# Issuing a transformer block's projections and FFN between the exponentials of its attention

## The chip, the cores and the metric

One core of one Trainium2 chip runs the whole block. The metric is device time in microseconds (us); lower is better. Executions of one kernel lay within about 0.5% of their median, and medians are quoted.

## The reference, cut to what matters

```python
B, S, D, H, F = 1, 2048, 512, 32, 1792        # head size 16, bf16 inputs
h  = x + attention(layernorm(x)) @ wo          # softmax over 2048 keys, 32 heads
h2 = h + (sigmoid(ln(h) @ w_gate) * (ln(h) @ w_up)) @ w_down
```

The scores are 32 x 2048 x 2048, and each needs one exponential. That is 2048 tiles of 128 keys by 512 queries, issued three at a time: 683 ScalarE instructions of 128x1536 elements (the last one shorter), in both kernels.

## The kernel before

Three stages follow each other. The first makes K, Q and V for everything, 128 rows at a time, through padded tiles and TensorE transposes. The second is attention (some lines cut):

```python
pt_next = emit_scores(groups[0])          # 3 score matmuls (K=32, row tiles), then exp -> pt
for gi, group in enumerate(groups):
    pt = pt_next
    if gi + 1 < len(groups):
        pt_next = emit_scores(groups[gi + 1])
    for ui, (qc, g, kt, j) in enumerate(group):
        nc.tensor.matmul(acc[32*j:32*j+32, :], lhsT=Vaug[:, kt, 4*g+j, :], rhs=pt[:, ui, :],
                         start=(kt == 0), stop=(kt == NT-1), tile_position=(0, 32*j))   # "AV"
        if kt == NT - 1 and j == 3:       # end of a head group's 512 queries: normalise
            nc.vector.tensor_copy(out=xs[:], in_=acc[:])
            nc.tensor.matmul(pr[:], lhsT=sel_f[:], rhs=xs[:], start=True, stop=True)    # fp32, L215
            nc.vector.reciprocal(out=rec[:], in_=pr[:])
            nc.gpsimd.tensor_tensor(out=QT[g][:, qs], in0=xs[:], in1=rec[:], op=ALU.mult)
```

On TensorE the order is: scores n+1, AV n, scores n+2, AV n+1. AV n needs exponential n. The third stage does the output projection and second layer norm of all rows and then the FFN, with `Sqrt` and `Sigmoid` on ScalarE; the trace shows the two partly interleaved.

## Time and profile before

| | before |
|---|---|
| time | 1452.25 us (4 runs, 1450.85 to 1453.69) |
| start to first exponential | 233.1 us |
| first to last exponential | 1011.2 us |
| last exponential to end | 204.8 us |
| mean TensorE clock between first and last exponential | 0.52 |

The prediction shows the lines behind this. The ends of the stages are start and end times of the exponentials' own records. In a row of the list of groups, the figures after the first bar are busy time and mean length of one instruction; those after the second are idle time just before and what ended it.

### The profile page before, as it was taken

The numbers are of one execution on the slowest core, as the hardware profiler recorded it, in microseconds if no ns is written. First come the engines' busy times: TensorE is split into PE (matmuls) and PEld (weight loads), VectorE is DVE, ScalarE is ACT, GpSimd is POOL, SyncE is SP. The second block draws the span as 40 slices with busy tenths as digits, with TensorE's granted clock in tenths as the row PEclk, the third lists the DMA queues.
The fourth block names the chain that finished last, engine by engine and source line by source line (L and its number), as shares of the span: only waits on it lengthen the run. The fifth ranks groups of instructions, "written<-read, shape, count | busy, mean of one in ns | idle before, by whom it ended". The sixth has DMA issues, their size and how long they took to land.

```text
span 1449.1 us, 13593 instructions
## 1 busy us (share of the span) xinstructions
PE 1142.7 (79%) x5512; PEld 358.9 (25%) x5539; DVE 323.8 (22%) x546; ACT 1054.5 (73%) x863; POOL 131.6 (9%) x128
## 2 busy tenths in 40 slices
PE   1665556888888888888888888888888888699998
PEld 0332222222222222222222222222222222234444
DVE  8533331111111111111111111111111111356433
ACT  1111116999999999899999989999998999456221
POOL 7442220000000000000000000000000000000000
PEclk9998765555555555555555555555555555699999
DMA  3000000000000000000000000000000000400000
GB/s 116 1 1 0 0 0 1 1 0 0 1 0 1 1 0 1 0 0 1 0 0 1 0 1 0 1 1 0 1 0 1 1 0 0 153 1 0 23 23 15
DMA packets 6670, 12.66 MB, mean 9 GB/s; under 512 B 400, under 2 KB 4496, under 8 KB 6608
## 3 DMA queue, kind: packets, MB, share of 16 engines
q1 hardware_dynamic: 4896, 6.03, 1.2%
q10 hardware_dynamic: 1056, 3.41, 0.7%
q0 software_dynamic: 656, 2.36, 0.6%
q8 instruction: 43, 0.70, 0.2%
q14 instruction: 19, 0.16, 0.0%
HBM read 9.70 MB, written 2.10 MB: 8 GB/s over the span
## 4 chain that ended last, share of the span: by engine, by line
ACT 59%; PE 27%; DVE 8%; issue 5%; POOL 1%; another core or an unknown queue 0%; ACTq 0%; DVEq 0%; POOLq 0%
ACT pt L193 56%; PE pm L113 5%; PE pr L215 5%; PE pm L263 3%; PE pf L251 3%; PE acc L206 3%; PE pf L254 3%; PE pm L228 2%; DVE xs L213 2%; POOL sq L120 1%; PE pss L189 1%; DVE sel_f L57 1%; PE pm L167 1%; PE pm L85 1%; DVE KT L87 1%
## 5 line engine op out<-in xcount | busy, mean ns | idle before, releaser
L193 ACT ACTIVATE pt<-pss 128x1536 bf16<-128x1536 f32 (+1 forms) x683 | 944.8, 1448 | 66.4 <-PE pss L189 66.4
L206 PE MATMUL acc<-pt,Vaug 128*32 128x512 bf16 x2048 | 418.3, 592 | 163.7 <-ACT pt L193 163.7
L189 PE MATMUL pss<-QT,KT 32*128 32x512 bf16 x2048 | 408.3, 592 | 0.7 <-ACT Vaug L172 0.7
L206 PEld LDWEIGHTS <-Vaug 128*32 128x32 bf16 x2048 | 133.4, 101 | 468.9 <-issue 468.9
L213 DVE COPY xs<-acc 128x512 f32<-128x512 f32 x32 | 22.1, 691 | 822.9 <-PE acc L206 822.9
L189 PEld LDWEIGHTS <-KT 32*128 32x128 bf16 x2048 | 71.7, 99 | 300.1 <-issue 299.2
L218 POOL TENSOR_TENSOR QT<-xs,rec 128x512 bf16<-128x512 f32 x32 | 40.4, 1264 | 961.0 <-DVE rec L217 961.0
L217 DVE RECIPROCAL rec<-pr 128x512 f32<-128x512 f32 x32 | 107.4, 3357 | 69.5 <-PE pr L215 69.5
L113 PE MATMUL pm<-wqkv_sb,xnT 128*128 128x512 bf16 x183 | 80.2, 599 | 17.1 <-DVE xnT L87 15.7
L257 ACT ACTIVATE sg<-pf 128x512 f32<-128x512 f32 x56 | 32.7, 596 | 70.1 <-PE pf L251 60.2
L215 PE MATMUL pr<-xs,sel_f 128*128 128x512 f32 x64 | 65.8, 1131 | 9.5 <-DVE xs L213 9.5
L75 ACT ACTIVATE rstd<-mv,eps_t 128x1 f32<-128x1 f32 x32 | 9.4, 294 | 78.4 <-DVE mv L73 78.3
L251 PE MATMUL pf<-xnT,wg 128*128 128x512 bf16 x219 | 58.8, 384 | 0.4
L167 PE MATMUL pm<-ident_bf,pad 128*128 128x128 bf16 x128 | 15.5, 297 | 54.0 <-DVE pad L162 54.0
L254 PE MATMUL pf<-xnT,wu 128*128 128x512 bf16 x221 | 57.6, 380 | 0.1
L263 PE MATMUL pm<-wd,hT 128*128 128x512 bf16 x219 | 48.4, 379 | 0.2
L85 PE MATMUL pm<-ident_bf,xn 128*128 128x128 bf16 x128 | 16.4, 267 | 39.6 <-DVE xn L78 39.4
L258 DVE TENSOR_TENSOR hT<-sg,pf 128x512 bf16<-128x512 f32 x56 | 38.2, 684 | 31.4 <-PE pf L254 27.0
L172 ACT CAST Vaug<-pm 128x512 bf16<-128x512 f32 x16 | 9.4, 585 | 48.4 <-PE pm L113 48.4
L120 POOL TENSOR_TENSOR sq<-pad 128x512 f32<-128x512 bf16 x32 | 33.2, 1038 | 95.5 <-ACT pad L155 50.6
L113 PEld LDWEIGHTS <-xnT 128*128 128x128 bf16 x192 | 24.7, 140 | 53.3 <-issue 32.6
L132 ACT CAST pad<-pm 128x512 bf16<-128x512 f32 x16 | 9.4, 585 | 38.0 <-PE pm L113 32.3
(57 smaller groups left out, 462.8 us busy)
## 6 DMA issues: line engine op xcount, KB each, us to landing
xb<-in_A_x_dram SPq DMA_DIRECT2D x1, 2048.0 KB, 12.5
out_dram<-ob SPq DMA_DIRECT2D x16, 128.0 KB, 1.7
wu<-in_B_w_up_dram ACTq DMA_DIRECT2D x1, 1792.0 KB, 15.8
wg<-in_B_w_gate_dram SPq DMA_DIRECT2D x1, 1792.0 KB, 17.2
wd<-in_B_w_down_dram POOLq DMA_DIRECT2D x1, 1792.0 KB, 17.7
wqkv_sb<-in_A_wqkv_dram ACTq DMA_DIRECT2D x1, 1536.0 KB, 10.0
wo_pad<-in_A_wo_dram POOLq DMA_DIRECT2D x4, 128.0 KB, 4.4
```

Of the source, the lines that this page charges most:

```text
L113: nc.tensor.matmul(ps[:], lhsT=xnT[:, c, t * P:(t + 1) * P], rhs=wqkv_sb[:, c, col0:col0 + D], start=(c == 0), stop=(c == DC - 1))
L120: nc.gpsimd.tensor_tensor(out=sq[:], in0=padded[:, :, 0:DH], in1=padded[:, :, 0:DH], op=ALU.mult)
L189: nc.tensor.matmul(pss[:, ui, :], lhsT=KT[32 * j:32 * j + 32, g, kt * P:(kt + 1) * P], rhs=QT[g][32 * j:32 * j + 32, qc * QC:(qc + 1) * QC ...
L193: nc.scalar.activation(out=pt[:, 0:n, :], in_=pss[:, 0:n, :], func=ACT.Exp, scale=DH ** -0.5)
L206: nc.tensor.matmul(acc[32 * j:32 * j + 32, :], lhsT=Vaug[:, kt, 4 * g + j, :], rhs=pt[:, ui, :], start=(kt == 0), stop=(kt == NT - 1), til ...
L213: nc.vector.tensor_copy(out=xs[:], in_=acc[:])
L215: nc.tensor.matmul(pr[:], lhsT=sel_f[:], rhs=xs[:], start=True, stop=True)
L217: nc.vector.reciprocal(out=rec[:], in_=pr[:])
L218: nc.gpsimd.tensor_tensor(out=QT[g][:, qs], in0=xs[:], in1=rec[:], op=ALU.mult)
L251: nc.tensor.matmul(psg[:], lhsT=wg[:, c, f * P:(f + 1) * P], rhs=xnT[:, c, qs], start=(c == 0), stop=(c == DC - 1))
L254: nc.tensor.matmul(psu[:], lhsT=wu[:, c, f * P:(f + 1) * P], rhs=xnT[:, c, qs], start=(c == 0), stop=(c == DC - 1))
L263: nc.tensor.matmul(psd[:], lhsT=hT[:, f, tt * P:(tt + 1) * P], rhs=wd[:, f, :], start=(f == 0), stop=(f == FC - 1))
```

## The change

The intent is to leave ScalarE nothing but exponentials, from as early to as late as possible, and to put the rest on the other engines beside them. The core of the diff, with cuts marked:

```diff
+    ctx.enter_context(tc.manual_schedule(engines={PE, Activation, DVE, Pool, SP}))  # program order
+    # ahead of the loop: layer norm, x^T, V for all rows, K of head group 0, Q of one tile
+    # "steps": generators that yield after about two matmuls
+    def prep_k(g):
+        for c in range(NQC):
+            ps = pm_tile()                      # one PSUM bank serves all background work
+            proj_T(ps, wk_pad, g, c)            # 4 matmuls
+            yield
+            evac_k(ps, g, c, False); sqs.append(square(...))
+        ...                                     # maximum of |k|^2, through small DMAs
+    def prep_q(qc, g): ...                      # projection made transposed, no TensorE transpose
+    def wo_ln(qc, alloc): ...                   # output projection, layer norm (Newton on DVE)
+    def ffn(qc):                                # gate 2+2 matmuls, tanh, up 2+2, multiply, down
+        nc.scalar.activation(out=th[:], in_=ps[:], func=ACT.Tanh, scale=0.5)    # sigmoid by tanh
     for n, group in enumerate(groups):
+        pss_next = scores(groups[n + 1])
+        nc.scalar.activation(out=pt[...], in_=pss[...], func=ACT.Exp, scale=DH ** -0.5)
+        av(GU if len(avq) <= 2 * GU else 2 * GU)    # AV of the group before, not of this one
+        for ui, u in enumerate(group):
+            avq.append((u, pt, ui))
+        step()                                      # one step of queued background work
+        finish()
-                    nc.vector.tensor_copy(out=xs[:], in_=acc[:])
-                    nc.tensor.matmul(pr[:], lhsT=sel_f[:], rhs=xs[:], start=True, stop=True)
-                    nc.vector.reciprocal(out=rec[:], in_=pr[:])
-                    nc.gpsimd.tensor_tensor(out=QT[g][:, qs], in0=xs[:], in1=rec[:], op=ALU.mult)
+        nc.vector.transpose(out=xs[...], in_=acc[:])       # 32x32 blocks: sums become a column
+        nc.vector.reciprocal(out=rec[:], in_=xs[:, :, DH:DH + 1])
+        nc.vector.tensor_tensor(out=o2[:, :, 0:DH], in0=xs[:, :, 0:DH], in1=rec[...], op=ALU.mult)
+        nc.vector.transpose(out=ot[:], in_=o2[...])
+    # after the loop: output projection and FFN of the last 512 rows alone
 ...
```

Besides, a new accumulator is never begun behind other AV matmuls of the same iteration (`av` returns early), and probabilities have four buffers instead of three.

## The prediction

> **What bounds the kernel now.** I read the page's forty slices first, then the busy time by stage, then the chain that ended last, then single instructions. The slices show three stages in sequence: ScalarE is nearly full only in the middle one, and the TensorE clock there stands at half.
>
> ```profile
> PE   1665556888888888888888888888888888699998
> DVE  8533331111111111111111111111111111356433
> ACT  1111116999999999899999989999998999456221
> PEclk9998765555555555555555555555555555699999
> ```
>
> Cutting the span where the exponentials (L193) begin and end gives the stages: 230 us of layer norm and projections, 1016 us of attention, 203 us of output projection and FFN. Columns are start:end, length, busy time (instructions) of PE, PEld, DVE, ACT, POOL, then clock, DMA share and GB/s.
>
> ```profile
> 0.00:230.40 230.40, 116.74 (x506) 55.13 (x515) 104.18 (x314) 37.09 (x80) 90.06 (x95) 0.86 0.06 19
> 230.40:1246.20 1015.80, 841.73 (x4162) 221.18 (x4163) 126.20 (x63) 947.36 (x686) 39.85 (x32) 0.52 0.00 1
> 1246.20:1449.10 202.90, 184.19 (x847) 82.59 (x862) 93.42 (x169) 70.01 (x98) 1.73 (x2) 0.96 0.11 38
> ```
>
> In the middle ScalarE is busy 947 of 1016 us, so it is the bound; in the outer stages it has 37 and 70 us of work and mostly waits. The group list names the work and the wait.
>
> ```profile
> L193 ACT ACTIVATE pt<-pss 128x1536 bf16<-128x1536 f32 (+1 forms) x683 | 944.8, 1448 | 66.4 <-PE pss L189 66.4
> L257 ACT ACTIVATE sg<-pf 128x512 f32<-128x512 f32 x56 | 32.7, 596 | 70.1 <-PE pf L251 60.2
> L75 ACT ACT_TABLE_LOAD x14 | 18.0, 1283 | 2.6 <-PEq L282 1.3 <-PE acc L206 1.2
> ```
>
> 683 exponentials occupy 944.8 us, 1.383 us each back to back (the 1448 ns counts their overlap). The 66.4 us before them comes once per head group of a query chunk: about 32 stalls of 2.1 us. One of them on ScalarE:
>
> ```profile
> 574.15 8.39 ACT L193 ACTIVATE pt<-pss 128x1536 bf16<-128x1536 f32 x6
> 584.56 5.48 ACT L193 ACTIVATE pt<-pss 128x1536 bf16<-128x1536 f32 x4 [2.02 <-PE pss L189]
> ```
>
> It is the fp32 matmul L215 that sums for the normalisation: 2.08 us on TensorE in program order, with the next scores behind it. Exact ends from the exponentials' own records: first start 233.1, last end 1244.3. So before = 233 + 1011 + 205 us.
>
> TensorE at half clock and at full clock, from three places: a tiled pair in attention, projection matmuls, FFN matmuls.
>
> ```profile
> 579.83 0.61 PE L206 MATMUL acc<-pt,Vaug 128*32 128x512 bf16 x2 [0.26 <-ACT pt L193]
> 580.37 0.61 PE L189 MATMUL pss<-QT,KT 32*128 32x512 bf16 x3
> ...
> 267.93 0.39 PE L189 MATMUL pss<-QT,KT 32*128 32x512 bf16 x3
> 268.25 0.40 PE L206 MATMUL acc<-pt,Vaug 128*32 128x512 bf16 x3
> ...
> 1299.96 1.03 PE L254 MATMUL pf<-xnT,wu 128*128 128x512 bf16 x4
> 1300.82 1.03 PE L251 MATMUL pf<-xnT,wg 128*128 128x512 bf16 x4
> ```
>
> Three tiled matmuls run side by side, and a set of three follows another at 0.54 us (half) or 0.32 us (full). A full-array matmul costs (1300.82 - 1299.96)/4 = 0.215 us at full clock and 0.43 at half (L113 loads its weights every 0.43 us).
>
> [...] The exponentials are at their rate and only their number could shrink, which the change leaves at 683. [...] 27 loads of 1283 ns while the layer norm's sqrt alternates with sigmoid. [...] TensorE busy some 80% in attention never lifts the clock by itself; it goes up for about 3.6 us after the dense stretch around L215 (267.6 to 271.2) and falls when TensorE is only about 60% busy. [...] 0.32 against 0.215 is 0.11 us for each change of mode. [...]
>
> **The change, part by part.** It keeps the attention arithmetic and weaves nearly everything else into it. Each of the 683 iterations issues scores one ahead, exp, an older AV, and one "step" of queued work (mostly two full-array matmuls).
>
> *Prologue, 233 to about 55 us.* Only layer norm, transposes, V, keys of head group 0 and one query tile remain ahead of the first exp. TensorE: 16 x 4 V + 4 x 4 K + 4 Q = 84 matmuls plus 64 transposes of about 0.12 us: 44 us at half clock, 26 at full. DVE: 16 tiles at roughly 0.66 + 0.18 + 0.5 + 0.2 us, 26 us in all. They overlap; the stream is dense, so I take 30 us. Before it 15 us: the load (the present one lands 12.5 us after issue, now in quarters), and DVE held up by GpSimd memsets as L57 is now for 17 us. After it about 9 us for maximum, two small DMAs of about 2 us, shift, first scores. Sum 54, call it 55: saves 178.
>
> *Exponential stage.* Floor 944.8 us. Added on ScalarE: tanh for three chunks, 3 x 14 = 42 at 0.596 = 25 us; no table switch, as the layer norm inside uses a Newton step on DVE. Removed: L215 and most of the 66 us. The normalisation becomes two 32x32 DVE transposes around a small reciprocal; the accumulator frees after the first, some 0.7 us as L213's copy takes 0.69, while TensorE has about an iteration of other work. Floor with tanh: 970.
>
> Whether TensorE fits under 970 is the disputed item. Background: 28 K and 31 Q projections of 4, 3 x 32 output projections, 3 x 168 FFN matmuls, 836 in all, and about 470 steps that add a change of mode. At half clock 683 x 2 x 0.54 = 738, plus 836 x 0.43 = 359, plus 470 x 0.11 = 52: 1149 us. At full 437 + 180 + 52 = 669. If each state holds half the time, 1/(0.5/1149 + 0.5/669) = 846. So TensorE fits on average when the full clock holds for over a quarter of the time. At half clock an iteration with background takes about 0.54 + 0.54 + 0.97 = 2.05 us, over 1.38, so TensorE becomes fully busy, which should lift the clock; at full clock it takes 1.18 us, 85%, which may or may not hold it. I expect alternation. The order of issue gives TensorE nearly an iteration of lead, which absorbs most of a slow window: [...] 0.11 us lost per iteration, but when late it is dense and the clock should stay up longer, so I take half: 470 x 0.055 = 26 us. About 4 more for steps with four matmuls and late normalisations: stage 1000, saves 11.
>
> *Tail, 205 to about 62 us.* Only the last chunk's part is exposed. Last AV and normalisation 3.5; output projection 4 x about 2.2 = 9; statistics, Newton (15 small DVE operations of about 0.17), apply and transposes 8; gate and up 14 x 8 x 0.215 = 24; down 56 x 0.215 = 12; a bubble, cold clock and the last store (1.7 us) 5.5. Saves 143.
>
> Sum: 55 + 1000 + 62 = 1117 us; I choose 1115, ratio 0.77. Nearly all of the gain is the two outer stages moved beside ScalarE; nothing makes the exponentials faster.
>
> **Rivals.** (a) TensorE holds full clock: only small stalls, stage 975, total about 1090. For it: the FFN stage holds 1.00 throughout once dense. Against it: the fall at about 60% busy, and the steps without matmuls that thin the stream. (b) TensorE stays at half clock and becomes the bound: stage about 1149, total 1266. For it: tiled matmuls at 80% busy never lift the clock. Against: that stream waits in every iteration; a saturated one would not. (c) The single background PSUM bank makes TensorE wait in order for DVE or tanh, so that scores arrive late: 14 x 3 x 2 evictions at up to 0.7 us is 59 us if wholly exposed, total about 1150. Against: an iteration's scores and AV lie between producer and reuse. (d) The 5.4 MB of FFN weights arrive late: the three loads now land in 15.8 to 17.7 us, and a third of a chunk (some 80 us) remains before their use. Negligible.
>
> **Range and chances.** Low end 1075: case (a) with a prologue and tail 15 us shorter. High end 1185: (c) in full, or half of (b). Even (b) in full is 13% below 1452, so slower would need a fault I don't see: faster 0.97, same 0.02, slower 0.01.
>
> **What would show it.** First exp at 45 to 70 us; last exp to end 55 to 70 us. The exp group again 945 us busy in 683, with idle before it well under 66 us. Clock in the middle stage 0.65 to 0.9 rather than 0.52; if it is 0.5, (b) is right, and exp waits for the scores throughout. Two or three table loads instead of 28. Wrong if the exp stage is over 1060 us, or if exp takes longer than 1.383 us each.

Its 0.11 us per iteration is an estimate that also follows from the times above: at equal shares of time an iteration takes 1/(0.5/2.05 + 0.5/1.18) = 1.498 us, 0.115 over the 1.383 taken for ScalarE. That half of it remains was my guess. That tanh needs no table load of its own was an assumption; the two loads of after bear it out.

What stands of the clock is measured in before. Between its first and last exponential it is full in 13 stretches, 44 us in all, each beginning within 5 us of the start of one of the 31 L215 there; TensorE is busy 53% in them (58% in the quoted one), and each time the clock fell again. Between two of them, from 271.3 to 363.3 us, TensorE is busy 85% at 0.50; in the FFN, from 1300 us on, 97% at 1.00. That a fuller stream lifts the clock was an expectation; a_fill2 shows it, 1.00 against 0.87. The cold clock of the tail is the 0.50 with which that stage begins, in after until 1031 us. The 0.11 us for a change of mode is a difference of measured times; in after, four full-array matmuls between two tiled sets take 0.96 us (108.18 to 109.14), 0.10 over 4 x 0.215. L57's four copies took 17.21 us and ended at 18.89, just behind GpSimd's memset of `Vaug` at 18.79. The two small DMAs were an estimate; in after the shift takes 1.8 us from its issue to the first scores (51.62 to 53.41), and the four copies of the maximum 3.8 us to their reader (46.58 to 50.38).

## The result, and the profile after

After: 1085.32 us (8 runs, 1081.40 to 1090.42); before, of the same rounds: 1452.75 us (13 runs). The ratio is 0.7474, interval 0.7462 to 0.7487. Ratios here are the mean time of one kernel's runs over that of the other's of the same rounds, so not quite the ratio of the medians.

The forty slices of after, to set against those of before:

```profile
PE   4687778787798877898788777897798777888878
DVE  6323333211114111012214111102224111110153
ACT  2488899999999999999999999999999999999811
PEclk9878998966658899899988999999878999995589
```

ScalarE is busy 80% or more from the third slice to the last but two. The clock is mostly high (0.87 in the middle stage), with two hollows, 0.62 from 217 to 326 us and 0.50 from 978 to 1027 us. The same three stages, cut at 54 and 1027 us (columns as in the prediction):

```profile
0.00:54.00 54.00, 28.65 (x156) 12.88 (x159) 26.19 (x75) 19.85 (x35) 24.14 (x22) 0.95 0.22 70
54.00:1027.20 973.20, 796.77 (x4964) 239.91 (x5032) 210.19 (x394) 945.70 (x725) 61.98 (x61) 0.87 0.04 11
1027.20:1086.60 59.40, 48.84 (x213) 21.90 (x217) 26.68 (x57) 8.36 (x15) 0.00 (x0) 0.90 0.03 9
```

| stage, us | before | predicted | after |
|---|---|---|---|
| to the first exponential | 233.1 | 55 | 54.1 |
| exponentials | 1011.2 | 1000 | 973.1 |
| after the last | 204.8 | 62 | 59.4 |

The group lines of the exponential, the tanh inside the loop, and one of the table loads:

```profile
L497 ACT ACTIVATE pt<-pss 128x1536 bf16<-128x1536 f32 (+1 forms) x683 | 938.7, 1650 | 31.9 <-PE pss L424 30.7
L359 ACT ACTIVATE th<-pm 128x512 f32<-128x512 f32 x42 | 35.8, 853 | 0.0
L497 ACT ACT_TABLE_LOAD x1 | 1.3, 1283 | 0.0
```

The idle time before the exponentials fell from 66.4 to 31.9 us. There are two table loads in the whole program (the other is for `Sqrt` at the start), against 28.

Busy times did not settle how far ScalarE is from its floor, since "busy" can hide lateness: the recorded length of an exponential has a median of 1450 ns in before and 1578 in after, more than it takes to the start of the next. So I took the start times of all 683 exponentials from each trace. Where nothing held one up, it started 1.331 us after the last in the kernel after. In the kernel before the distances alternate between two values, 1.35 and 1.42 us; their mean is the 1.383 that the prediction took for ScalarE's own rate. A tanh between two exponentials makes the distance 1.808, so it costs 0.477. Below, **lateness** is the sum of all distances beyond 1.331 (and beyond 0.477 for a tanh): 102.4 us before, 44.1 after.

So the gain of 362 us in the two profiled executions is 179 ahead of the exponentials, 145 behind them, and 38 within: 58 of lateness less 20 for 42 tanh.

### The profile page after: what moved, and what is told of

Its sections match the earlier page's. It is cut to its first block, busy times and chain, and to the rows that moved or that the text cites. A ratio compares the mean times of both kernels' runs of the same rounds, so it can differ in the third digit from the quotient of the medians.

```text
span 1086.6 us, 13171 instructions
## 1 busy us (share of the span) xinstructions
PE 874.3 (80%) x5328; PEld 274.7 (25%) x5408; DVE 263.1 (24%) x526; ACT 973.9 (90%) x774; POOL 86.1 (8%) x82
## 4 chain that ended last, share of the span: by engine, by line
ACT 48%; issue 23%; PE 22%; DVE 5%; POOL 1%; DMA 1%; ACTq 0%; DVEq 0%
ACT pt L497 45%; PE pss L424 5%; PE pm L146 5%; PE acc L452 4%; ACT th L359 3%; PE pss L530 2%; DVE KT L155 1%; PE pss L539 1%; PE b L200 1%; PE pm L353 1%; DVE st L109 1%; PE pss L323 1%; PE b L119 1%; PE pm L119 0%; DVE xn L113 0%
## 5 line engine op out<-in xcount | busy, mean ns | idle before, releaser
L497 ACT ACTIVATE pt<-pss 128x1536 bf16<-128x1536 f32 (+1 forms) x683 | 938.7, 1650 | 31.9 <-PE pss L424 30.7
L424 PE MATMUL pss<-qt,KT 32*128 32x512 bf16 x2048 | 303.0, 431 | 161.5 <-ACT pt L497 137.0
L452 PE MATMUL acc<-pt,Vaug 128*17 128x512 bf16 x2048 | 306.2, 434 | 1.4 <-DVE xs L433 1.1
L424 PEld LDWEIGHTS <-KT 32*128 32x128 bf16 x2048 | 113.1, 93 | 424.0 <-issue 409.3
L452 PEld LDWEIGHTS <-Vaug 128*17 128x17 bf16 x2048 | 65.6, 88 | 189.4 <-issue 189.4
L160 POOL TENSOR_TENSOR sq<-qt 128x512 bf16<-128x512 bf16 x32 | 33.3, 1041 | 627.8 <-DVE qt L186 627.8
L353 PE MATMUL pm<-hnT,wg 128*128 128x512 bf16 x155 | 49.4, 394 | 4.9 <-DVE hT L368 3.6
L363 PE MATMUL pm<-hnT,wu 128*128 128x512 bf16 x153 | 49.3, 397 | 0.0
L146 PE MATMUL pm<-xnT,wq_pad 128*128 128x512 bf16 x104 | 41.1, 473 | 2.5 <-issue 2.5
L160 POOL TENSOR_TENSOR sq<-KT 128x512 bf16<-128x512 bf16 x32 | 33.3, 1040 | 79.5 <-DVE KT L155 52.8
L359 ACT ACTIVATE th<-pm 128x512 f32<-128x512 f32 x42 | 35.8, 853 | 0.0
```

Source lines behind the costliest of these rows:

```text
L146: nc.tensor.matmul(ps[:], lhsT=w_pad[:, d, 4 * g:4 * g + 4, :].rearrange("p h r -> p (h r)"), rhs=xnT[:, d, c * QC:(c + 1) * QC], start=(d ...
L160: nc.gpsimd.tensor_tensor(out=sq[:], in0=src, in1=src, op=ALU.mult)
L353: nc.tensor.matmul(ps[:], lhsT=wg[:, d, f * P:(f + 1) * P], rhs=hnT[:, d, :], start=(d == 0), stop=(d == DC - 1))
L359: nc.scalar.activation(out=th[:], in_=ps[:], func=ACT.Tanh, scale=0.5)
L363: nc.tensor.matmul(ps[:], lhsT=wu[:, d, f * P:(f + 1) * P], rhs=hnT[:, d, :], start=(d == 0), stop=(d == DC - 1))
L424: nc.tensor.matmul(pss[:, ui, :], lhsT=KT[g][32 * j:32 * j + 32, kt * P:(kt + 1) * P], rhs=QT[qc, g][32 * j:32 * j + 32, :], start=True, s ...
```

## The experiments

All outputs are right. Times of the edits of before are set against 1452.0 us in the same rounds, those of the first set of edits of after against the unchanged kernel run beside them.

| run | us | ratio to before | exponential stage | lateness | its clock |
|---|---|---|---|---|---|
| before | 1452.75 | 1 | 1011.2 | 102.4 | 0.52 |
| b_avlate | 1437.40 | 0.9895 | 996.2 | 87.2 | 0.51 |
| b_ring4 | 1454.41 | 1.0013 | 1014.1 | 105.3 | 0.52 |
| b_dvenorm | 1386.81 | 0.9549 | 949.1 | 40.4 | 0.50 |
| b_both | 1369.03 | 0.9428 | 931.1 | 22.1 | 0.50 |
| after | 1085.32 | 0.7474 | 973.1 | 44.1 | 0.87 |
| a_again | 1088.41 | 0.7489 | 975.8 | 46.8 | 0.86 |
| a_ksplit | 1069.95 | 0.7373 | 954.1 | 25.1 | 0.89 |
| a_fill2 | 1072.85 | 0.7386 | 958.6 | 29.7 | 1.00 |
| a_ksplit_fill2 | 1058.02 | 0.7286 | 943.9 | 15.0 | 0.99 |
| a_ksplit_fill1 | 1057.10 | 0.7276 | 940.8 | 11.8 | 1.00 |
| a_avearly | 1179.07 | 0.8113 | 1064.5 | 135.7 | 0.82 |
| a_ffn2late | 1122.74 | 0.7725 | 965.3 | 43.0 | 0.79 |
| a_prepfront | 1217.18 | 0.8376 | 962.3 | 33.3 | 0.81 |

**What made the lateness before? Three edits of the kernel before.** Theory: part is the fp32 matmul L215 in TensorE's order, part is the order "AV n ahead of scores n+2" at half clock. Rivals: 1.383 is ScalarE's own rate; or the ring of three probability buffers.

AV one group later (with four buffers):

```diff
-        pt_next = emit_scores(groups[0])
-        for gi, group in enumerate(groups):
-            pt = pt_next
+        lagged = [None] + groups
+        pts = [None, emit_scores(groups[0])]
+        for gi, group in enumerate(lagged):
             if gi + 1 < len(groups):
-                pt_next = emit_scores(groups[gi + 1])
+                pts.append(emit_scores(groups[gi + 1]))
+            if group is None:
+                continue
+            pt = pts[gi]
```

> The kernel before with the AV matmuls issued one group of three later (and four probability buffers instead of three). Theory 1 (before, each AV waits for the exponential just finished and stands ahead of the next scores, so at half clock every second exponential starts some 85 ns late): the spacing of exponentials falls from a mixture of 1.34 and 1.42 us to 1.33 to 1.34 throughout, 682 x 0.045 = 31 us, and part of each 2.1 us stall at a head group's end goes too; 1390 to 1422 us. Theory 2 (1.38 us is ScalarE's own spacing in this program, or set by the ring of three buffers): 1447 to 1457 us for the former; the run with four buffers alone tells the latter.

Four buffers alone, `bufs=3` to `bufs=4`:

> The kernel before with four probability buffers instead of three and nothing else. Theory 1 (order of AV and scores): no change, 1447 to 1457 us, spacing still alternating 1.34 and 1.42. Theory 2 (the ring of three holds every second exponential): spacing 1.33 to 1.34, about 1420 us.

The normalisation of after in place of L213 to L218 (the four lines of the diff above, writing `QT[g][:, qs]`):

> The kernel before with only the normalisation of the kernel after (DVE transpose, small reciprocal, multiply, transpose back) in place of copy, fp32 matmul L215, wide reciprocal and GpSimd multiply. If the fp32 matmul in TensorE's program order makes the 2.1 us stall, 32 stalls shrink to below 0.4 us each: 55 to 66 us less, 1387 to 1398 us. Rival, the wait for the accumulator to be emptied makes it: about half stays, 1415 to 1435 us.

TensorE in before, in the middle of a head group:

```profile
599.81 0.61 PE L206 MATMUL acc<-pt,Vaug 128*32 128x512 bf16 x3 [0.26 <-ACT pt L193]
600.36 0.61 PE L189 MATMUL pss<-QT,KT 32*128 32x512 bf16 x3
601.15 0.62 PE L206 MATMUL acc<-pt,Vaug 128*32 128x512 bf16 x3 [0.19 <-ACT pt L193]
601.70 0.61 PE L189 MATMUL pss<-QT,KT 32*128 32x512 bf16 x3
602.58 0.62 PE L206 MATMUL acc<-pt,Vaug 128*32 128x512 bf16 x3 [0.26 <-ACT pt L193]
```

AV starts 1.34 and then 1.43 us apart, each released by an exponential. The scores behind it finish 0.55 + 0.61 = 1.16 us after AV started, nearly the whole of ScalarE's 1.33. With AV later (b_avlate) the scores are released by the exponential, AV follows them, and all scores start evenly:

```profile
600.39 0.61 PE L189 MATMUL pss<-QT,KT 32*128 32x512 bf16 x3 [0.18 <-ACT pt L193]
600.93 0.61 PE L209 MATMUL acc<-pt,Vaug 128*32 128x512 bf16 x3
601.74 0.61 PE L189 MATMUL pss<-QT,KT 32*128 32x512 bf16 x3 [0.19 <-ACT pt L193]
602.28 0.62 PE L209 MATMUL acc<-pt,Vaug 128*32 128x512 bf16 x3
603.08 0.61 PE L189 MATMUL pss<-QT,KT 32*128 32x512 bf16 x3 [0.18 <-ACT pt L193]
```

In b_avlate 651 of 682 distances are 1.33 to 1.35, at an unchanged half clock; with four buffers alone the alternation stays. So 1.383 was not ScalarE's rate, and the ring didn't make it: the order of issue did, at half clock. Before itself agrees: in 20 distances that fell wholly in full-clock moments it shows no 1.42. Why it is every second one, and not each, I did not find out. The time was a miss, 1437 instead of 1390 to 1422: of the 32 us of lateness outside the stalls 0.4 were left, but all 31 stalls at the ends of head groups grew, from 2.3 us of lateness on average to 2.8, and took back half. L215 still stands in the way, and the expected relief there did not come. Why they grew was not tested.

b_dvenorm removed those stalls: 65 us, at the upper end of its 55 to 66. The exponentials' group in this run, to set against the 66.4 us of the kernel before:

```profile
L193 ACT ACTIVATE pt<-pss 128x1536 bf16<-128x1536 f32 (+1 forms) x683 | 945.4, 1448 | 3.7 <-PE pss L189 3.7
```

The first DVE transpose frees the accumulator after 0.72 us, no sooner than the copy L213 did (0.69), so the rival, the wait for the accumulator, is out; what went is the normalisation's part on TensorE. Of the ends, 11 keep 0.4 to 0.5 us, and the alternation stayed.

Both edits together:

> The kernel before with both the later AV and the normalisation on DVE. If the middle stage before is 683 exponentials at 1.331 us, plus 36 us of lateness from the order of issue at half clock, plus 66 us of stalls from L215, both go and it falls from 1011 to about 912 us: 1345 to 1358 us in all. If the two savings are of the same time, it stays near 1385.

1369 us, 11 over the range: they add up in direction, but 22 us of lateness remain, 0.9 to 1.2 us at 21 of the ends. TensorE and DVE at one of them in b_both:

```profile
263.77 0.61 PE L213 MATMUL acc<-pt,Vaug 128*32 128x512 bf16 x1
...
264.41 0.72 DVE L220 STREAM_TRANSPOSE xs<-acc 128x512 f32<-128x512 f32 x1 [34.50 <-PE acc L213]
264.57 0.58 PE L189 MATMUL pss<-QT,KT 32*128 32x512 bf16 x1 [0.19 <-ACT pt L193]
...
265.18 0.61 PE L213 MATMUL acc<-pt,Vaug 128*32 128x512 bf16 x2
...
265.73 0.60 PE L189 MATMUL pss<-QT,KT 32*128 32x512 bf16 x2
```

The head group ends in the middle of an AV set of three. The new accumulator's two AV wait for the transpose, and two of the next three scores wait behind them. The kernel after puts the new accumulator's AV into the next iteration, behind the scores; this edit lacks that. This is read from the trace and not tested by a run, but the count fits: with 64 tiles to a head group and sets of three, 21 of the 31 ends fall inside a set, and just these are late.

**What makes the lateness after? Two edits of the kernel after, and the unchanged one beside them.**

> The kernel after, unchanged, as the measure for the three that run beside it on the same chip: 1080 to 1091 us.

K and first-Q projections in steps of two matmuls (and, in the first chunk, the next chunk's Q queued last):

```diff
-            proj_T(ps, wk_pad, g, c)
+            proj_T(ps, wk_pad, g, c, 0, 2)
+            yield
+            proj_T(ps, wk_pad, g, c, 2, 4)
             yield
...
```

> The kernel after with its K and first Q projections issued in steps of two matmuls instead of four (and the next chunk's Q work queued behind them in the first chunk). In the first query chunk the trace of after shows 24 us of lateness between exponentials beyond 1.33 us each, in steps that are 0.54 us late at full clock and about 1.0 at half. If the four-matmul steps make it, about two thirds goes: 10 to 20 us less than the unchanged kernel. Rival (the lateness comes from waits for DVE evictions of the one background bank, or from the clock alone): within 4 us, or slower.

ScalarE and TensorE in after, in the first chunk, at full clock from 107 us on:

```profile
107.77 1.45 ACT L497 ACTIVATE pt<-pss 128x1536 bf16<-128x1536 f32 x1 [0.38 <-PE pss L424]
109.64 1.45 ACT L497 ACTIVATE pt<-pss 128x1536 bf16<-128x1536 f32 x1 [0.42 <-PE pss L424]
```
```profile
107.27 0.39 PE L424 MATMUL pss<-qt,KT 32*128 32x512 bf16 x3
107.59 0.39 PE L452 MATMUL acc<-pt,Vaug 128*17 128x512 bf16 x3
108.18 1.02 PE L146 MATMUL pm<-xnT,wk_pad 128*128 128x512 bf16 x4 [0.20 <-DVE KT L155]
109.14 0.39 PE L424 MATMUL pss<-qt,KT 32*128 32x512 bf16 x3
```

With four matmuls the iteration takes 109.14 - 107.27 = 1.87 us, 0.54 too long. The split took 18 us off, within the expected 10 to 20; lateness in the first chunk fell from 24.5 to 6.9. The edit also moved the next chunk's Q in the queue; but by the start times the exponentials behind the 28 K steps were 16.4 us late in the unchanged kernel and 0.9 here, so the split did it.

Two idle matmuls ahead of the scores wherever the last step had none, written into the PSUM that the scores then overwrite (the lines that count matmuls are cut):

```diff
+        for r in range(heat["k"]):          # 2 after a step without matmuls, else 0
+            nc.tensor.matmul(pss[:, 0, :], lhsT=ident_bf[:], rhs=xnT[:, r, 0:QC], start=True, stop=True)
         for ui, (qc, g, kt, j) in enumerate(group):
```

> The kernel after with two idle full-array matmuls ahead of the scores in each iteration whose background step had no matmul, so that the stream does not thin. If thin iterations let the clock fall, and the slow windows after them make the lateness, mean clock of the exponential stage rises from about 0.88 to over 0.95 and 10 to 25 us go. Rival (lateness is made by the steps and waits themselves): clock rises but the time stays within 5 us, or grows since scores come later.

The clock in the stage went to 1.00 and 15.6 us went. Distances wholly at half clock were 146 of 682 with 20.6 us of lateness in the unchanged kernel, and 2 here. So thin iterations do let the clock fall, and the slow stretch then makes exponentials late. The four-matmul steps stay late, up to 0.54 us each at full clock: 15 of the 29.7 us that remain come behind them.

> The kernel after with both edits, the split K steps and two idle matmuls in thin iterations. If one removes the lateness of four-matmul steps and the other that of slow windows, lateness falls from 44 us to 10 to 15: 1050 to 1060 us, clock of the stage 0.99. Rival (both remove the same stalls): 1066 us or more.

> The same with one idle matmul in place of two. If the clock is held by how full TensorE's stream is, one may not do: clock between 0.90 and 0.99 and time between that of the split alone (1070) and that of split with two (1050 to 1060).

1058.0 and 1057.1 us: the two savings are nearly all of different time (2.0% of before together, 1.2 and 1.0% apart). One idle matmul holds the clock as well as two (1.00 and 0.99). The stages of the version with one:

```profile
0.00:56.20 56.20, 31.64 (x159) 13.77 (x159) 26.27 (x75) 19.91 (x36) 24.32 (x22) 0.96 0.21 67
56.20:997.00 940.80, 805.94 (x5296) 236.09 (x5295) 209.88 (x394) 938.34 (x725) 61.95 (x61) 1.00 0.04 11
997.00:1055.50 58.50, 47.85 (x218) 21.43 (x217) 26.69 (x57) 8.36 (x15) 0.00 (x0) 0.94 0.03 10
```

It beats both kernels: 1057.10 against 1085.32 and 1452.15 us. What is left in its middle stage is 683 exponentials at 1.331 us, 20 us of tanh and 12 of lateness.

**What is the overlap itself worth? Three edits that undo one part.**

AV behind its own exponential, as in before:

```diff
-        av(GU if len(avq) <= 2 * GU else 2 * GU)
         for ui, u in enumerate(group):
             avq.append((u, pt, ui))
+        av(2 * GU)
```

> The kernel after with the AV of a group issued behind its own exponential, as in the kernel before. Theory: the later AV is what gives background steps their room, since now AV waits for the exponential and the background stands between it and the next scores; in each of some 470 steps the scores come 0.1 to 0.3 us late: 40 to 150 us slower, spacing 1.45 us and more in steps with matmuls. Rival (TensorE has room at full clock either way): within 15 us.

94 us slower than after. ScalarE and TensorE of this run:

```profile
399.71 5.85 ACT L497 ACTIVATE pt<-pss 128x1536 bf16<-128x1536 f32 x4
...
402.75 0.39 PE L452 MATMUL acc<-pt,Vaug 128*17 128x512 bf16 x3 [0.27 <-ACT pt L497]
...
403.08 0.60 PE L353 MATMUL pm<-hnT,wg 128*128 128x512 bf16 x2
...
403.61 0.39 PE L424 MATMUL pss<-qt,KT 32*128 32x512 bf16 x3
```

The exponential releases AV, then the background runs, then the scores: 403.61 - 402.75 + 0.39 = 1.25 us from release to scores, and the four exponentials stand (5.85 - 1.45)/3 = 1.47 apart. So the later AV, which cost nothing to write, is what makes room for background work.

The FFN of the third chunk after the loop instead of in it:

> The kernel after with the FFN of the third query chunk taken out of the attention loop and run after it. If work beside ScalarE is free but for its tanh, the time grows by the 168 matmuls at 0.215 us = 36 us and 1 to 3 us of bubbles, less 14 tanh of 0.48 us = 7 and at most 3 us of lateness: 25 to 32 us. Rival (TensorE is the bound in the loop too, so work only moves): 0 to 12 us.

34 us slower than the unchanged kernel beside it, a little over the 25 to 32. The last stage grew by 101.8 - 57.9 = 43.9, and the exponential stage shrank by 975.8 - 965.3 = 10.5 (14 tanh at 0.477 are 6.7 of that). So one chunk's FFN costs 44 us in the open and 10.5 in the loop. The clock of the stage fell to 0.79, yet lateness did not grow (43.0 us against 46.8). Without background work half clock was enough: in after, from 977 to 1020 us, the clock is 0.50, and 32 exponentials there are 0.6 us late together.

The preparation of head groups 1 to 7 ahead of the loop:

```diff
+    while bg:
+        step()
     units = [(qc, g, kt, j) for qc in range(NQC) ...]
```

> The kernel after with the K and first Q projections of the other seven head groups run before the attention loop instead of beside it. In the open each group takes its 20 matmuls and, through the one background bank, four K evictions, a maximum, a small DMA and the Q shift in sequence, about 13 to 16 us, 90 to 110 in all; in the loop they cost only the lateness of the first chunk, some 20 of 24 us. Net 70 to 95 us slower, first exponential at 145 to 165 us. Rival (the loop pays for them nearly in full): under 30 us slower.

132 us slower than the median of after; I had expected 70 to 95. The first exponential came at 194.2 us, so each group took 140/7 = 20 us, not 13 to 16. Between 54 and 200 us TensorE was busy for 80.5 of 146 us and the clock was 0.50: by the 0.43 and 0.215 us of one, 20 matmuls take 8.6 us there instead of 4.3. The direction held, the size of the chain did not.

How the 179 and 145 us ahead of and behind the exponentials divide between moving work and making it cheaper was not tested in full. This run puts 140 of the 179 back. Behind, one chunk takes 59 us in after, and a quarter of before's 205 is 51, so no gain from cheaper work shows there.

## Why the prediction was right or wrong

The range held: 1115 forecast, 1075 to 1185, and 1085 measured. The picture of three stages with the outer two moved beside ScalarE is what happened, and two terms came within 3 us: prologue 55 against 54.1, tail 62 against 59.4. The middle came out 27 us below its 1000 by errors of opposite sign:

- **"The exponentials are at their rate and only their number could shrink" was the step that failed.** The term 944.8 us should have been 683 x 1.331 = 909; of the 36 us between, 32 are the alternation. What misled me: exponentials that look back to back in the page (1448 ns each, overlapping) can each be late by less than the overlap. The alternation of 1.34 and 1.43 was to be seen in before's own timeline. b_avlate showed the order of issue at half clock to be the cause; after starts 36 us lower there than the prediction had it.
- **Tanh**: 25 us forecast from 596 ns each; 42 x 0.477 = 20 measured, since a tanh, 853 ns long as recorded, overlaps its neighbours.
- **Lateness**: 30 us forecast, 44 measured. More than half, 24 us, fell in the first chunk. I had listed "about 4 more for steps with four matmuls and late normalisations"; a_ksplit shows that splitting those steps was worth 18. Such steps come four in a row, and in a_fill2, at full clock, the last three are mostly 0.54 us late each. The 470 steps were a little too many as well: the trace has 433 with matmuls, which would make the 26 us 24.
- **Clock**: I took half the time at each level. Of the 682 distances 494 lay wholly at full clock and 142 at half, mean 0.87, inside the 0.65 to 0.9 given. That it alternates, and that slow stretches cost time nearly only where background work stands, after, a_fill2 and a_ffn2late bear out: in after, of the distances wholly at half clock, 46 with background work are 15.9 us late together and the others 2.2.
- **L215's stall**: named rightly, and b_dvenorm gives it by itself: 65 us.
- **Rivals**: (a), about 1090 with a stage of 975, hit the number, but not for its reason, since the clock didn't hold; a_fill2, where it does hold, still has 29.7 us of lateness. (b) did not occur. (c) is not excluded for parts of what remains: the DVE wait of 0.20 us in the lines above is one, small; a_ksplit_fill1, with the same single bank, has 11.8 us of lateness in all, so it is at most that there, of the 59 named. (d): no exponential waited on a DMA in any list of waits I looked at; not tested by a run.
- **Table loads**: the prediction read 27 where `Sqrt` alternates with `Sigmoid`; of the 28, 26 lie there. Nothing rests on it.

In all, the failed step was a rate read off an average. The number was saved by the size of the outer stages, where the sums held.

## What to carry to other kernels

Where one engine is the floor, take its rate from the start-to-start times of single instructions where nothing stands before them (1.331 us here), not from busy time divided by count (1.383). Then order the feeding engine so that what the bound engine needs next goes first and what only consumes its results follows later; this order decided 94 us here before any background work was tuned. When other work is woven in, cut it so that every iteration fits within the floor at the clock that it will get (four matmuls at once made it 1.87 us against 1.33, at full clock), and keep the stream full enough to hold that clock, if need be with an idle matmul (0.89 in a_ksplit, 1.00 with one in a_ksplit_fill1).
